# When the second piece of q and the first weight slice are sent for, in a fused attention and SwiGLU kernel

## The chip, the cores and the metric

The kernel runs on one core of a Trainium2 chip. The metric is the device time of one execution in microseconds (us), and the median of several executions is what kernels are compared by. The profile shows one execution in detail.

## The reference

Attention without a softmax over pairs: q is normalised along its 64 features, k along the sequence, and the two products are taken with the small matrix in the middle. The result, as 4608 tokens of 512 features, goes through a SwiGLU block.

```python
# q, k, v: (8 batches, 8 heads, 576 positions, 64 features), float32
q_s = softmax(q, axis=features);  k_s = softmax(k, axis=positions)
kv  = einsum('bhsd,bhse->bhde', k_s, v)
x   = einsum('bhsd,bhde->bhse', q_s, kv)        # -> (4608, 512)
g   = x @ w_gate                                # (512, 1536)
out = (g * sigmoid(g) * (x @ w_val)) @ w_out    # (1536, 512), float32 out
```

## The kernel before

**Tiling.** The eight heads of a batch are two groups (G = 0 and 1) of four. One load brings q, k or v of one batch and group into a tile of 128 partitions with 2 x 576 float32 each (576 KB). Positions are cut into nine steps of 64; `A` is steps 0 to 4 and `Z` is steps 5 to 8. For batch 0 alone, q is loaded in these two pieces: first A (320 KB a group), later Z (256 KB a group). The weights `wg`, `wv` and `wo` are cast to float16 as they are loaded. `wg` and `wv` come in four slices of columns each: 256, 256, 512 and 512 wide. I call the eight slices w0 to w7 in the order of issue: w0 is the first of `wg`, w1 the first of `wv`, w2 the second of `wg`, and so on. The list `w_dma` of the code holds them.

**Queues.** The order on every engine is written by hand (`tc.manual_schedule()`), and each engine takes its instructions in that order. All loads of q, k and v are issued by SyncE, one after the other, on one hardware queue (q1 in the profile). The weight slices are issued by GpSimd on a software queue (q0), since they are cast on the way. Both queues are served by the same 16 DMA engines. `load(b, G, what, src, after, t0, t1)` issues one load; if `after` is given, SyncE waits until that other transfer has landed before it issues this one. `tc.add_manual_dep(a, b, ...)` does the same for any pair of instructions.

**The start.** SyncE issues, with nothing to wait for: q piece A for both groups, k and v of group 0, k and v of group 1, q piece Z for both groups. GpSimd waits for k of group 0 to land and then issues w0 to w7 one behind the other. SyncE's next load, q of batch 1, waits for w5.

While this comes in, TensorE is kept running by products of zeros (`warm_up`). ScalarE takes the exponential of q's piece A (line 129, tile `eq`) and of k (line 129, tile `ek`); VectorE and GpSimd normalise q (`rs`, `rr` at lines 148 and 153, `qs` at line 160); TensorE transposes q (line 176, `tp` copied to `qt`), forms `kv` (line 200) and then `x` (line 245, `xp`), which is copied to `xt` as the input of the SwiGLU block.

**The first chunk.** `PLAN_0` is a string of steps that says what every engine does next. It begins:

```
zq0 zs0 zq1 zs1 zn1* M00 zn0 N00 M10 N10 M20 zt0* M30 zt1 zx0 zx1 N20 N30 M01 M11
```

`zq0` and `zq1` are the exponentials of q's piece Z for group 0 and 1, on ScalarE. `zs` are its sums (VectorE), `zn` the multiplications (`zn1*` on VectorE, `zn0` on GpSimd), `zt` the transposes (`zt0*` is copied by ScalarE, `zt1` by VectorE), and `zx` the products with `kv`. `Mm0` is the gate product (`g_ps`, line 318) of the weight columns 128 m to 128 m + 127 with the tokens of piece A, followed by a Silu on ScalarE (`sg`, line 331); `Nm0` is the value product (`u_ps`, line 318) followed by a multiplication on VectorE (`hr`, line 336). `Mm1` and `Nm1` are the same for the tokens of piece Z. So M00 needs w0, N00 needs w1, M20 needs w2, N20 needs w3, and M01 needs what `zx` made. The name `psp` is the pool of eight banks of PSUM that all products share.

**Afterwards** come seven chunks of 512 tokens. TensorE runs their products (lines 398, 451, 489 and 543) nearly without a pause. `w_out` comes in four slices: two of them wait for w6, two (step `wo` of the plan) for v of batch 1.

Of the kernel before, what the change touches and what calls it, by code (L numbers as in the profile page):

```python
# [12 lines left out]
SYNC = mybir.DependencyInfo(mybir.DependencyClass.Sync, mybir.DependencyReason.DATA)  # L13
# [3 lines left out]
def kernel(  # L17
# [59 lines left out]
    dmas = {}  # L77
    raw = {}

    def load(b, G, what, src, after=None, t0=0, t1=T):  # L80
        if t0 == 0:
            raw[what, b, G] = ld.tile(
                [128, 2, T * 64], FP32, tag=what, name=what, bufs=3 if what == "q" else None
            )
        ap = bass.AP(
            tensor=src.tensor,
            offset=src[b, 4 * G].offset + 64 * t0,
            ap=[[T * 64, 128], [2 * HSTR, 2], [1, 64 * (t1 - t0)]],
        )
        d = nc.sync.dma_start(out=raw[what, b, G][:, :, 64 * t0:64 * t1], in_=ap)  # L90
        if after is not None:
            tc.add_manual_dep(d.ins, after.ins.name, SYNC, reason="order of loads")
        dmas[what, b, G] = d
# [5 lines left out]
    def w_slice(dst, src, c0, n):  # L99
        ap = bass.AP(  # L100
            tensor=src.tensor,
            offset=src[0, c0].offset,
            ap=[[d_ff, 128], [128 * d_ff, KT], [1, n]],
        )
        return nc.gpsimd.dma_start(out=dst[:, :, c0:c0 + n], in_=ap)
# [17 lines left out]
    A, Z = BANKS = ((0, 5), (5, 9))  # L123
# [488 lines left out]
    with tc.manual_schedule():  # L612
# [3 lines left out]
            load(0, G, "k", k)  # L616
            load(0, G, "v", v)
        for G in range(NG):
            load(0, G, "q", q, None, *Z)
        warm = const.tile([128, 1], FP32, name="warm", tag="warm")  # L620
        nc.vector.memset(warm, 0.0)
        nc.scalar.activation(out=warm, in_=warm, func=AF.Exp)
# [14 lines left out]
        w_dma = []  # L637
        for c0, n in ((0, 256), (256, 256), (512, 512), (1024, 512)):
            w_dma.append(w_slice(wg, moe_w_gate, c0, n))
            w_dma.append(w_slice(wv, moe_w_val, c0, n))  # L640
        tc.add_manual_dep(w_dma[0].ins, dmas["k", 0, 0].ins.name, SYNC, reason="order of loads")
        load(1, 0, "q", q, after=w_dma[5])
        load(1, 1, "q", q)

# [205 lines left out]
```

## Time and profile before

| what | us |
|---|---|
| median of 6 runs | 297.14 |
| lowest and highest of these | 296.86 and 299.57 |
| the profiled execution, its time | 297.63 |
| the profiled execution, its span | 295.6 |
| TensorE busy in the span | 284.9 (96%) |
| VectorE busy | 236.7 (80%) |
| ScalarE busy | 216.2 (73%) |
| GpSimd busy | 149.2 (50%) |

The span runs from the first to the last instruction of the core; the time holds some 2 us more that lie around it. Times in a view are counted from the start of the span. In the profile PE is TensorE, PEld its weight loads, ACT is ScalarE, DVE is VectorE, POOL is GpSimd, and SPq is SyncE's issuing of DMAs. An arrow `<-` in a group's name stands between what is written and what is read; an arrow in front of an engine names what ended its waiting.

### The profile page before, as it was taken

How to read it: one execution, taken by the hardware profiler on the slowest of the kernel's cores; microseconds unless marked ns; L12 is line 12 of the kernel's file. 1: busy time of each engine (PE TensorE's matmuls, PEld its weight loads, DVE VectorE, ACT ScalarE, POOL GpSimd, SP SyncE). 2: the span in 40 equal slices, each digit the busy share in tenths (PEclk: the TensorE clock that was granted, in tenths of full speed). 3: DMA queues.
4: the chain of work that ended last, by engine and by line, in shares of the span. 5: the costliest groups of instructions: out<-in, count | busy, mean ns of one | idle time of the engine just before them, and what ended most of it. 6: DMA issues, size and time to landing. Idle time of an engine off the chain costs nothing.

```text
span 295.6 us, 7115 instructions
## 1 busy us (share of the span) xinstructions
PE 284.9 (96%) x2708; PEld 233.3 (79%) x2708; DVE 236.7 (80%) x523; ACT 216.2 (73%) x401; POOL 149.2 (50%) x128
## 2 busy tenths in 40 slices
PE   8889999799999999999999999999999999999993
PEld 6658775577888878887888788878887888888882
DVE  3475797598998889888988898889888798677791
ACT  4674896798896799669966997599758766677421
POOL 2813688466329722972197219730973255344300
PEclk9999999999999999999999999999999999999999
DMA  7999999757906970698059805990570000510065
GB/s 220 323 201 246 283 329 268 250 109 193 358 12 147 265 295 0 133 252 321 1 121 249 335 4 122 225 357 2 111 113 2 2 2 0 109 35 2 0 145 142
DMA packets 39425, 46.46 MB, mean 157 GB/s; under 512 B 16352, under 2 KB 23008, under 8 KB 39392
## 3 DMA queue, kind: packets, MB, share of 16 engines
q1 hardware_dynamic: 33408, 41.03, 49.1%
q0 software_dynamic: 5824, 4.72, 10.3%
q8 instruction: 21, 0.34, 0.5%
q10 hardware_dynamic: 160, 0.26, 0.2%
q14 instruction: 12, 0.10, 0.1%
HBM read 37.75 MB, written 9.44 MB: 160 GB/s over the span
## 4 chain that ended last, share of the span: by engine, by line
PE 83%; DMA 10%; DVE 2%; POOL 2%; ACT 1%; issue 1%; SPq 0%; ACTq 0%; DVEq 0%
PE sx L398 24%; PE ox L543 13%; PE sw L398 12%; PE ow L543 6%; PE sy L398 6%; DMA wo<-in_moe_w_out_dram 5%; PE oy L543 4%; PE g_ps L318 3%; PE u_ps L451 3%; PE g_ps L451 3%; PE u_ps L318 3%; DMA wv<-in_moe_w_val_dram 3%; PE kv L200 2%; DMA k<-in_k_dram 2%; PE o_ps L489 1%; POOL qs L160 1%
## 5 line engine op out<-in xcount | busy, mean ns | idle before, releaser
L398 PEld LDWEIGHTS <-gt 128*128 128x128 f16 x672 | 65.3, 98 | 10.8 <-issue 0.6
L433 POOL TENSOR_TENSOR hr<-sg,u 128x512 bf16<-128x512 f16 (+1 forms) x32 | 36.6, 1144 | 73.1 <-ACT sg L424 47.7
L117 ACT COPY s<-sx 128x512 f32<-128x512 f32 (+1 forms) x70 | 40.7, 581 | 17.0 <-PE sx L398 16.9
L398 PE MATMUL sx<-xs,gt 128*128 128x256 f16 (+1 forms) x336 | 49.9, 271 | 0.1
L442 POOL TENSOR_TENSOR hr<-sg,u 128x512 bf16<-128x512 f16 (+1 forms) x32 | 36.5, 1141 | 23.5 <-ACT sg L441 23.5
L543 PEld LDWEIGHTS <-hs 128*128 128x128 bf16 x384 | 37.4, 98 | 5.5
L437 DVE TENSOR_TENSOR u<-sx,s 128x512 f16<-128x512 f32 (+1 forms) x42 | 28.5, 679 | 12.9 <-PE sx L398 5.6
L398 PEld LDWEIGHTS <-wg 128*128 128x128 f16 x336 | 32.4, 98 | 5.2 <-issue 0.2
L160 POOL TENSOR_TENSOR qs<-eq,rr 128x1152 bf16<-128x1152 bf16 (+2 forms) x15 | 30.7, 2052 | 11.3 <-DVE rr L153 7.7
L432 DVE TENSOR_TENSOR u<-sw,s 128x512 f16<-128x512 f32 (+1 forms) x42 | 28.5, 679 | 7.5 <-PE sw L398 7.3
L441 ACT ACTIVATE sg<-sx 128x512 f16<-128x512 f32 (+1 forms) x42 | 25.0, 596 | 10.8 <-PE sx L398 10.0
L424 ACT ACTIVATE sg<-s 128x512 f16<-128x512 f32 (+1 forms) x42 | 26.6, 632 | 6.8 <-DVE s L422 6.7
L543 PEld LDWEIGHTS <-hr 128*128 128x128 bf16 x288 | 28.2, 98 | 3.3
L422 DVE TENSOR_TENSOR s<-sy,s 128x512 f32<-128x512 f32 (+1 forms) x42 | 27.8, 661 | 2.5 <-PE sy L398 1.3
L117 ACT COPY s<-sw 128x512 f32<-128x512 f32 (+1 forms) x36 | 21.0, 582 | 6.1 <-PE sw L398 5.8
L398 PE MATMUL sy<-xt,wg 128*128 128x256 f16 (+1 forms) x168 | 24.9, 271 | 0.1
L148 DVE TENSOR_REDUCE rs<-eq 128x18 f32<-128x1152 bf16 (+2 forms) x18 | 21.7, 1203 | 4.2 <-ACT eq L129 4.2
L398 PE MATMUL sx<-xt,wg 128*128 128x256 f16 (+1 forms) x168 | 25.0, 271 | 0.0
L398 PE MATMUL sw<-xs,gt 128*128 128x256 f16 (+1 forms) x168 | 24.9, 271 | 0.0
L398 PE MATMUL sx<-xt,gt 128*128 128x256 f16 (+1 forms) x168 | 24.9, 271 | 0.0
L398 PE MATMUL sw<-xs,wv 128*128 128x256 f16 (+1 forms) x168 | 24.7, 271 | 0.0
L543 PE MATMUL ox<-wt,hs 128*128 128x256 f16 x192 | 23.6, 273 | 0.0
(107 smaller groups left out, 548.9 us busy)
## 6 DMA issues: line engine op xcount, KB each, us to landing
k<-in_k_dram SPq DMA_DIRECT2D x16, 576.0 KB, 7.4
v<-in_v_dram SPq DMA_DIRECT2D x16, 576.0 KB, 8.0
out_dram<-o_sb SPq DMA_DIRECT2D x70, 128.0 KB, 2.4
q<-in_q_dram SPq DMA_DIRECT2D x14, 576.0 KB, 7.0
wo<-in_moe_w_out_dram POOLq DMA_DIRECT2D x4, 384.0 KB, 9.0
wg<-in_moe_w_gate_dram POOLq DMA_DIRECT2D x2, 512.0 KB, 12.3
wv<-in_moe_w_val_dram POOLq DMA_DIRECT2D x2, 512.0 KB, 14.8
q<-in_q_dram SPq DMA_DIRECT2D x2, 320.0 KB, 3.5
```

The source lines that it names most:

```text
L117: nc.scalar.copy(out=out, in_=in_)
L148: nc.vector.reduce_sum(out=s["rs"][:, r], in_=s["eq"].rearrange("p t h d -> p (t h) d")[:, r], axis=mybir.AxisListType.X,)
L160: eng.tensor_mul(s["qs"].rearrange("p t (h d) -> p (t h) d", d=64)[:, r], s["eq"].rearrange("p t h d -> p (t h) d")[:, r], s["rr"][:, r].t ...
L398: nc.tensor.matmul(out=bank[:, h * j:h * j + h], lhsT=wgt(kk, j), rhs=rhs[:, kk, 0:h], start=first and j == 0 and kk == 0, stop=kk == 1, s ...
L422: nc.vector.tensor_add(self.s1, self.y[:, 0:w], self.s1)
L424: nc.scalar.activation(out=self.sa[:, 0:w], in_=self.s1, func=AF.Silu)
L432: nc.vector.tensor_add(u, self.w[:, 0:w], self.s2)
L433: meng.tensor_mul(self.out(0), self.halves(self.sa), self.halves(u))
L437: nc.vector.tensor_add(self.u, self.x[:, 0:w], self.s5)
L441: nc.scalar.activation(out=sb[:, 0:w], in_=self.x[:, 0:w], func=AF.Silu)
L442: meng.tensor_mul(self.out(1), self.halves(sb), self.halves(self.u))
L543: nc.tensor.matmul(out=dst[p][:, 0:HN], lhsT=lhs(kk, p), rhs=rhs(kk), start=start and i == 0, stop=i == HM - 1, skip_group_check=True,)
```

## The change

Two triggers are changed. SyncE now issues q's piece Z of group 0 only when k of group 1 has landed; the piece Z of group 1 follows in SyncE's order. GpSimd issues w0, and with it the seven slices behind it, when v of group 0 has landed, where it was k of group 0. The order of the instructions on each engine is unchanged, and so is every transfer.

```diff
@@ load order of batch 0 @@
             load(0, G, "k", k)
             load(0, G, "v", v)
         for G in range(NG):
-            load(0, G, "q", q, None, *Z)
+            load(0, G, "q", q, dmas["k", 0, 1], *Z)
...
-        tc.add_manual_dep(w_dma[0].ins, dmas["k", 0, 0].ins.name, SYNC, reason="order of loads")
+        tc.add_manual_dep(w_dma[0].ins, dmas["v", 0, 0].ins.name, SYNC, reason="order of loads")
```

## The prediction

> **What bounds the kernel now.** I read the page first. TensorE is busy for 96% of the span, and in the chain that ended last it holds 83%, DMA 10%. So a change of two load triggers can matter only where TensorE still waits for loads, near the start. I therefore took the chain of waits over the first 24 us, in order of time (start, duration, what):
>
> ```profile
> 1.75 5.98 DMA k<-in_k_dram
> ...
> 8.04 0.93 POOL wg L105
> 8.97 7.66 DMA wv<-in_moe_w_val_dram
> 16.62 0.05 issue
> 16.67 0.72 PE u_ps L318 x4
> 17.39 0.54 PE g_ps L318 x4
> ```
>
> The reader is to see that the end is set through k of group 0, then w0's issue, then w1's landing at 16.62, then N00 on TensorE. From there the chain stays on TensorE with no piece of DMA until 41.39, where a slice of `w_out` comes in. What is late at 16.67 is thus late at the end, unless something behind it has room.
>
> Next the timeline of ScalarE around that point (start, duration, group, idle before and its releaser), since the exponentials of q's piece Z stand ahead of the first Silu:
>
> ```profile
> 15.10 0.42 ACT L117 CAST xt<-xp 128x320 f16<-128x320 f32 x1 [0.67 <-PE xp L245]
> 15.42 1.15 ACT L129 ACTIVATE eq<-q 128x512 bf16<-128x512 f32 x2
> 16.59 1.28 ACT L331 ACT_TABLE_LOAD   x1
> 17.88 0.77 ACT L331 ACTIVATE sg<-g_ps 128x320 f16<-128x320 f32 x2
> 19.05 0.44 ACT L331 ACTIVATE sg<-g_ps 128x320 f16<-128x320 f32 x1 [0.41 <-PE g_ps L318]
> 19.39 0.58 ACT L117 COPY qt<-tp 128x512 bf16<-128x512 bf16 x1
> ```
>
> Neither exponential waits for its data now: the pieces land 9.4 and 10.1 us after their issues at 3.80 and 4.31, at 13.2 and 14.4, and are wanted at 15.42 and about 16.0. ScalarE's only slack behind them is the 0.41 ahead of 19.05.
>
> Last, GpSimd, and the DMAs by stretches of one us (the last two columns are the DMA share and GB/s):
>
> ```profile
> 8.04 0.94 POOL L105 DMA_DIRECT2D wg<-in_moe_w_gate_dram  x1 [0.73 <-DMA k<-in_k_dram]
> ...
> 13.36 0.80 POOL L105 DMA_DIRECT2D wv<-in_moe_w_val_dram  x1
> 17.16 1.04 POOL L160 TENSOR_TENSOR qs<-eq,rr 128x512 bf16<-128x512 bf16 x1 [3.00 <-DVE rr L153]
> ```
>
> ```profile
> 11.00:12.00 1.00, 1.00 (x19) 0.82 (x14) 0.58 (x3) 1.00 (x1) 1.00 (x3) 1.00 1.09 368
> 12.00:13.00 1.00, 0.73 (x8) 0.26 (x5) 0.56 (x3) 0.90 (x4) 1.00 (x2) 1.00 1.33 257
> 13.00:14.00 1.00, 0.88 (x21) 0.76 (x22) 0.59 (x4) 0.39 (x2) 1.00 (x2) 1.00 1.41 207
> 26.00:27.00 1.00, 1.00 (x11) 0.80 (x9) 0.94 (x3) 0.73 (x3) 0.00 (x0) 1.00 1.24 206
> 27.00:28.00 1.00, 1.00 (x11) 0.83 (x9) 0.42 (x2) 0.68 (x2) 0.71 (x1) 1.00 1.19 281
> ```
>
> The GB/s are bytes written. Near 390 means float32 loads of k, v and q; near 206 means weights, whose float16 writes are half of what is read. The change of rate shows who is served: weights begin only near 11.7 although w0 was issued at 8.04, that is, when the loads queued ahead of them are nearly through. The engines are busy throughout, so the change can only reorder this work or open a hole in it.
>
> **The triggers.** k of group 1 is issued at 2.77 and takes 8.1: the first Z load moves from 3.80 to about 10.95 and the second to about 11.45, by the 0.51 between two of SyncE's issues. SyncE's next load, q of batch 1, waits for w5 until 24.2 anyway, so nothing else is held up in its queue. v of group 0 is issued at 2.26 and takes 7.2, so it is there at 9.45 (ScalarE's cast starts then), where k was there at 7.73. All eight weight issues move by 1.7 us, and the last ends near 15.9 instead of 14.16. What stands behind them on GpSimd is zn0 at 17.16, after 3.00 idle: that covers it with 1.3 to spare. Without the cover it would cost TensorE's transposes the excess.
>
> **What does not get better.** k and v of both groups are ahead of the Z loads in one queue, and weights flow only near 11.7, when k of group 1 (10.9) has landed and v of group 1 (3.29 + 9.1 = 12.4) nearly has. So taking the Z loads and the weights out of their way buys nothing that I can find in these rows.
>
> **Step 1, w1 and N00.** Upper end: the 7.66 us from issue to landing stays, w1 lands at 18.3, and N00 is 1.7 late. Lower end: weights start as soon as v of group 1 is drained, hence near 11.7 as before, and the 512 KB of q (1.3 us at 390) are no longer all ahead of them; w1 could be 1.3 earlier, but TensorE waits only 0.67 there, so -0.67. I take the middle, +0.5: the queue that kept the weights from starting is gone earlier, but there is a hole, since k and v run out near 11.7 to 12.4 while q's first bytes can't come before about 12.3 (the first load is issued at 0.74 and bytes flow in the stretch from 2 to 3). M00, which needs w0, isn't the tighter one: its last operand from `xt` comes at 15.62.
>
> **Step 2, the Z loads.** They now arrive at engines that hold queued weights. The nearest row is the pair of q loads of batch 1, issued at 24.22 and 24.70 into queued w6 and w7. The rate stays at 206 until 27, so first bytes come some 3.0 us after the issue; the second load takes 8.1 and lands at 32.8. That is 1152 KB in the remaining 5.6 us, or 206 KB/us, half the unloaded rate. For 512 KB: 10.95 + 3.0 + 2.5 = 16.45. I add one small slice's time, 0.75 us of issue, since slices are queued here once per 0.75 us but land only every 1.35 (w2 at 9.71 + 8.1, w3 at 10.44 + 8.7), so that the queue is still growing. So the second piece lands near 17.2 where zq1 would have started at 16.0: 1.2 late. ScalarE takes its work in order; the table load, the first Silus and the copy of `qt` behind zq1 are all 1.2 late, less the 0.41 of slack, and zx0 on TensorE, which stands right behind that copy, is 0.8 late. Bounds: 14.7 to land (the 320 KB load at 0.74 took 3.3 us unloaded), which costs nothing; or the 8.1 us of the row unscaled, 19.55, which makes 3.55 late and costs 3.1.
>
> The Trainium skill, page "DMA: Bandwidth & Descriptors", section on queues, rings and completion order, says that an engine alternates between queues a packet at a time, about 9 to 17 descriptors. By that rule the q pieces would share evenly from 12.3 on and take an estimated 2.6 us, to 14.9, and step 2 would cost nothing. The row at 24.22, with its 3 us without a byte of q, speaks against so short a wait, though 206 KB/us afterwards fits an even share.
>
> **The sum.** Both steps delay the same engine and don't add up: the larger counts. Step 1 gives +0.5, step 2 gives +0.8, so +0.8. All later loads follow from landings or from TensorE's own progress and move along. The profiled execution would go from 297.63 to 298.4 (span 295.6 to 296.4); it lies 0.5 above the median of 297.14, so the median becomes 297.9.
>
> **Rivals.**
> - *The Z pieces are held behind the weights* (slower). The queue of slices keeps q out for longer than the row at 24.22 shows. For: the weights are issued first, and ScalarE can't pass zq1. Against: in that row q got its half once it started. If q lands with w3, 19.1 + 0.5, zq1 is 3.6 late and TensorE 3.2: 300.3. It decides from a landing of the second piece at about 17.9, where the loss passes 1.5. Chance 0.25.
> - *The weights keep their latency* (slower). Step 1's upper end, +1.7: 298.8. For: nothing in this trace shows a weight slice starting sooner after its issue. Against: the work queued ahead explains that start. Chance 0.13.
> - *Everything hidden*: the pieces share evenly, w1 lands where it did: 297.1 to 297.5. Chance 0.12.
> - *The weights gain* (faster): N00 loses its wait of 0.67, 296.5. Beyond that only the 1.83 us that TensorE waits at 54.83 for `w_out` could go too, if the later loads fall better: 294.6. Against: the second needs an order of transfers that the change doesn't touch. Chance 0.11, of which 0.06 passes the bound below.
>
> The forecast itself has 0.39, with its own range of 297.3 to 298.7.
>
> **How the numbers follow.** A difference of 0.5%, 1.5 us, is about what a measurement of this kernel can tell from no change. Faster by more: 0.06. Slower by more: all of the first rival, most of the second (0.11), and the forecast's upper edge (0.08), together 0.44. Within: 0.50. For the range I leave out the gain beyond 296.6 (about 0.08) and the part of the first rival beyond 300.2 (about 0.12).
>
> **What would show it.** In the profile of the changed kernel: the w0 issue at about 9.75; q's Z issues near 10.95 and 11.45; ScalarE waiting before `eq` for a DMA of q, which it does not now; N00 at 16.7 to 18.3; and the same distance from N00 to the end. I am wrong if `eq` has no wait and N00 comes no later than 16.67, if the Z pieces land after 18, or if the distance from N00 to the end changes by over 0.5 us.

## The result, and the profile after

The changed kernel takes 298.77 us (median of 28 runs, 296.85 to 301.89), the kernel before 297.12 (65 runs). The ratio is 1.0049, with a 95% interval of 1.0034 to 1.0064: slower by 1.5 us, which lies so near to the 0.5% that was called the bound of no change that the interval can't say on which side. The ratio leaves out the few executions that took over 1.5% more than the fastest of the same kernel; the two medians, which are 1.65 us apart, do not. The profiled execution took 299.21 with a span of 297.2; before it was 297.63 and 295.6.

The chain of waits of the changed kernel (start, duration, what) no longer runs over w1 and N00. It runs over k of group 1, SyncE, and q's second piece:

```profile
2.77 8.66 DMA k<-in_k_dram
...
11.46 0.37 SPq L90
11.82 0.04 issue
11.87 7.32 DMA q<-in_q_dram
19.18 0.02 issue
19.21 0.63 ACT eq L129
19.84 0.02 issue
19.85 1.28 ACT L331
21.14 0.01 issue
21.15 1.09 ACT sg L331 x3
22.24 0.49 ACT qt L117
22.73 0.04 issue
22.77 0.42 PE xp L245 x8
23.19 1.19 PE u_ps L318 x8
```

The last line is N20, which began at 20.83 before: 2.36 late. The chain of the kernel before had this from there on:

```profile
20.83 1.19 PE u_ps L318 x8
...
36.58 1.06 ACT sg L331 x3
37.64 3.00 POOL qs L160
40.64 0.74 POOL wo L113
41.39 13.40 DMA wo<-in_moe_w_out_dram
54.83 0.81 PE o_ps L489 x3
```

ScalarE's timeline shows the waits that were not there before, 0.59 and 1.70 ahead of the two exponentials of piece Z:

```profile
15.86 0.42 ACT L117 CAST xt<-xp 128x320 f16<-128x320 f32 x1 [0.67 <-PE xp L245]
16.88 0.63 ACT L129 ACTIVATE eq<-q 128x512 bf16<-128x512 f32 x1 [0.59 <-DMA q<-in_q_dram]
19.21 0.63 ACT L129 ACTIVATE eq<-q 128x512 bf16<-128x512 f32 x1 [1.70 <-DMA q<-in_q_dram]
```

zq1 starts at 19.21 instead of 16.0. On TensorE N00 is late too, but the chain does not run over it:

```profile
18.04 0.72 PE L318 MATMUL u_ps<-xt,wv 128*128 128x320 f16 x4 [1.26 <-DMA wv<-in_moe_w_val_dram]
...
22.77 0.42 PE L245 MATMUL xp<-qt,kn 64*64 64x256 bf16 x8 [0.80 <-ACT qt L117]
```

GpSimd issues w0 at 10.28, 2.2 later than before. Of this 1.7 is the trigger. The rest is not the change's: the first loads, issued at the same times in both, landed later here. ScalarE's start on k of group 0 is at 8.48 instead of 7.75 (between 7.5 and 8.7 in the profiles of this study), on v of group 0 at 10.00 instead of 9.45, and on k of group 1 at 11.46 instead of 10.93. So about 0.5 us of all the times above belong to this one execution.

Later in the chain a part is given back at the wait for `w_out`:

```profile
43.02 0.75 POOL wo L113
43.77 12.64 DMA wo<-in_moe_w_out_dram
56.41 0.04 issue
56.45 0.81 PE o_ps L489 x3
```

GpSimd's issue is 2.38 later than before (40.64), but the slice takes 12.64 instead of 13.40 to land, and TensorE goes on at 56.45 instead of 54.83, 1.62 later. That is what is left at the end of the span, 1.6.

### The profile page after: what moved, and what is told of

Its sections match the earlier page's. It is cut to its first block, busy times and chain, and to the rows that moved or that the text cites. A ratio compares the mean times of both kernels' runs of the same rounds, so it can differ in the third digit from the quotient of the medians.

```text
span 297.2 us, 7114 instructions
## 1 busy us (share of the span) xinstructions
PE 286.1 (96%) x2708; PEld 233.6 (79%) x2708; DVE 236.9 (80%) x523; ACT 216.2 (73%) x401; POOL 149.2 (50%) x128
## 4 chain that ended last, share of the span: by engine, by line
PE 81%; DMA 10%; DVE 2%; ACT 2%; POOL 1%; SPq 1%; issue 0%; ACTq 0%; DVEq 0%
PE sx L398 24%; PE ox L543 13%; PE sw L398 12%; PE ow L543 6%; PE sy L398 6%; DMA wo<-in_moe_w_out_dram 4%; PE oy L543 4%; PE u_ps L451 3%; PE g_ps L451 3%; DMA k<-in_k_dram 3%; PE g_ps L318 3%; DMA q<-in_q_dram 2%; PE u_ps L318 2%; PE kv L200 2%; PE o_ps L489 1%; POOL qs L160 1%
## 5 line engine op out<-in xcount | busy, mean ns | idle before, releaser
L148 DVE TENSOR_REDUCE rs<-eq 128x18 f32<-128x1152 bf16 (+2 forms) x18 | 21.8, 1210 | 6.0 <-ACT eq L129 6.0
```

Source lines behind the costliest of these rows:

```text
L148: nc.vector.reduce_sum(out=s["rs"][:, r], in_=s["eq"].rearrange("p t h d -> p (t h) d")[:, r], axis=mybir.AxisListType.X,)
```

## The experiments

Two theories stood at the start. Theory Z: the loss is ScalarE's wait for q's second piece, which the weights hold back. Theory W: the loss is that the weights come later. All kernels below are compared with the kernel before, run on the same chip.

**The q trigger alone.** The weights are issued on k of group 0, as before.

```diff
-            load(0, G, "q", q, None, *Z)
+            load(0, G, "q", q, dmas["k", 0, 1], *Z)
```

> The q trigger alone; the weights are issued on k of group 0 as before. Theory Z (the loss is ScalarE's wait for q's second piece, held back by weights queued in the DMA engines): the weights are queued even earlier than in the changed kernel, so the piece lands at 18 or later, ScalarE waits 2 us or more before its exponential of group 1, and the loss is all there: 298.3 to 299.3, 0.4 to 0.7% over before. Theory W (the loss is the later issue of the weights): N00 on TensorE starts at 16.7 or earlier and the time is that of before, 297.1, or up to 0.6 less.

Measured: 300.19 us (6 runs), ratio 1.0089 (1.0057 to 1.0120). The second piece lands 7.9 us after its issue, at 18.9, and ScalarE waits for both pieces. N00 starts at 15.73, 0.94 earlier than before, so the weights gain and the kernel loses: theory W falls. But the loss is larger than the changed kernel's although zx0 is no later (22.50). The stretches of one us of this run show why; the third column from the right is the clock granted to TensorE:

```profile
20.00:21.00 1.00, 0.70 (x8) 0.53 (x8) 0.93 (x3) 0.99 (x2) 0.25 (x1) 1.00 1.23 204
21.00:22.00 1.00, 0.64 (x6) 0.33 (x5) 0.90 (x3) 1.00 (x4) 0.00 (x0) 0.88 1.25 208
22.00:23.00 1.00, 0.50 (x8) 0.25 (x7) 0.56 (x3) 0.82 (x3) 0.00 (x0) 0.50 1.24 207
23.00:24.00 1.00, 1.00 (x8) 0.59 (x5) 0.75 (x2) 0.61 (x2) 0.00 (x0) 0.50 1.23 203
...
27.00:28.00 1.00, 1.00 (x7) 0.69 (x6) 0.00 (x0) 0.40 (x2) 0.35 (x1) 0.50 1.25 209
28.00:29.00 1.00, 1.00 (x8) 0.78 (x7) 0.13 (x1) 0.37 (x1) 1.00 (x2) 0.70 1.13 316
```

TensorE paused 1.93 us ahead of zt0 and 0.80 ahead of zx0, and from about 21.8 to 28.6 it has half its clock. Five of the six executions had a mean clock of 0.988 to 0.992 and took 299.4 to 300.9; the sixth kept 0.999 and took 297.5. I had not thought of this.

**The weight trigger alone.**

```diff
-        tc.add_manual_dep(w_dma[0].ins, dmas["k", 0, 0].ins.name, SYNC, reason="order of loads")
+        tc.add_manual_dep(w_dma[0].ins, dmas["v", 0, 0].ins.name, SYNC, reason="order of loads")
```

> The weight trigger alone; q's second piece is issued at 3.8 as before. Theory Z: the piece lands by 14.5, ScalarE has no wait for it, and the time is within 0.25% of before, 296.7 to 297.7, with N00 at 16.7 to 17.3. Theory W: N00 comes 1.4 us later than before, at 18.0, and the time is 298.5, all of the change's loss.

Measured: 297.08 us (12 runs), ratio 0.9989 (0.9966 to 1.0013): no loss, as theory Z has it. The profile, of the slowest of the twelve (299.46), has N00 at 18.20, 1.53 later than before, but its first loads were 0.9 late; that leaves some 0.6 for the trigger, which does not show in the median. This interval lies wholly below the changed kernel's (1.0034 to 1.0064). The two kernels differ in q's trigger alone, so the loss needs that trigger.

**Both triggers on v of group 0.** q's second piece is issued some 1.5 us earlier than in the changed kernel; the weights stay as changed.

```diff
-            load(0, G, "q", q, dmas["k", 0, 1], *Z)
+            load(0, G, "q", q, dmas["v", 0, 0], *Z)
```

> Both triggers on v of group 0: q's second piece now waits for the same landing as the weights, 1.5 us earlier than in the changed kernel. Theory Z: its bytes start about 1.3 us after SyncE's issue, near 10.8, ahead of the first weight bytes near 11.7, so the pieces land by 14 to 15, ScalarE has no wait, and the time is 297.0 to 297.6. Theory W: the weights are as late as in the changed kernel and the time is 298.5.

Measured: 297.86 us (12 runs), ratio 1.0021 (1.0001 to 1.0041), a little above what was expected of theory Z and well below the 298.5 of W. Its interval and the changed kernel's overlap slightly. The pieces are issued at 9.29 and 9.7 and land 4.0 and 4.5 us later, ahead of the weights; ScalarE runs both exponentials without a wait:

```profile
15.48 1.15 ACT L129 ACTIVATE eq<-q 128x512 bf16<-128x512 f32 x2
```

So a second piece that was issued at 9.7, beside w0 (9.58), took 4.5 us, and one that was issued at 11.87, 1.6 behind w0 (10.28), took 7.3.

**The changed kernel without the wait.** The exponential reads the steps of piece A instead.

```diff
-            in_=raw[what, b, G].rearrange("p h (t d) -> p t h d", d=64)[:, t0:t1],
+            in_=raw[what, b, G].rearrange("p h (t d) -> p t h d", d=64)[:, t0 % 5:t0 % 5 + t1 - t0],
```

> The changed kernel, but the exponential of q's second piece reads the first piece's steps instead, so it waits for no late load; all transfers stay, and only the numbers of positions 320 to 575 of batch 0 differ. Theory Z: the wait at 19.2 is gone, zx0 on TensorE goes back to within 0.3 us of N00's own lateness, and at most the lateness of N00 is left: 297.3 to 298.0. Theory W: nothing changes, 298.5.

Measured: 299.09 us (6 runs), ratio 1.0068 (1.0044 to 1.0093). Both theories missed: with the wait gone the kernel is no faster. TensorE's timeline shows what took its place:

```profile
15.21 1.02 PE L318 MATMUL g_ps<-xt,wg 128*128 128x320 f16 x4
18.36 1.25 PE L318 MATMUL u_ps<-xt,wv 128*128 128x320 f16 x4 [2.12 <-DMA wv<-in_moe_w_val_dram]
19.40 1.27 PE L318 MATMUL g_ps<-xt,wg 128*128 128x320 f16 x4
20.46 1.27 PE L318 MATMUL u_ps<-xt,wv 128*128 128x320 f16 x4
21.53 0.76 PE L318 MATMUL g_ps<-xt,wg 128*128 128x320 f16 x4
```

After a pause of 2.12 us the same four products take 1.25 us instead of 0.72, until 21.7. The granted clock, again the third column from the right, is half meanwhile:

```profile
18.00:19.00 1.00, 0.65 (x3) 0.41 (x4) 0.94 (x2) 0.53 (x2) 0.43 (x1) 0.60 1.42 196
19.00:20.00 1.00, 1.00 (x6) 0.52 (x5) 0.29 (x1) 0.00 (x0) 0.00 (x0) 0.50 1.28 206
20.00:21.00 1.00, 1.00 (x6) 0.52 (x5) 0.20 (x1) 0.29 (x1) 0.00 (x0) 0.50 1.26 205
21.00:22.00 1.00, 1.00 (x7) 0.64 (x6) 0.16 (x1) 0.14 (x1) 0.00 (x0) 0.69 1.24 201
```

This called for a third theory, C: a pause of some 2 us costs TensorE its clock, and a part of the loss is that.

**Theory C, three kernels.** A step `wu` issues products of zeros, as the kernel's own `warm_up` does, where TensorE would pause.

In the changed kernel (the kernel that ran has nine products ahead of N00, where the expectation says eight):

```diff
-... M00 zn0 N00 M10 N10 M20 zt0* M30 zt1 zx0 ...
+... M00 wu9 zn0 N00 M10 N10 M20 zt0* M30 zt1 wu6 zx0 ...
```

> The changed kernel with products of zeros in TensorE's pauses: 8 (0.86 us at full clock) between M00 and N00 and 6 ahead of zx0. Theory C (a part of the change's loss is TensorE's clock, which falls to half for some microseconds in those executions where the pauses last long enough): no execution has a mean clock under 0.995 any more, and the time falls by 0.3 to 1.0 us against the changed kernel, to 297.7 to 298.4. Rival (the loss is the waits alone): 298.6 as the changed kernel.

Measured: 298.83 us (9 runs), ratio 1.0072 (1.0042 to 1.0101). The mean clock was 0.994 to 0.999, so it was kept, but the time did not fall: for the changed kernel theory C fails, and its loss is not mainly the clock. Its own runs say the same: of the 27 executions in the ratio, nineteen had a mean clock of 0.994 or more and a median of 298.45, and eight had 0.990 to 0.993 and a median of 298.98. In this profile the second piece lands at 19.4 and zx0 starts at 23.02, behind the same chain as in the changed kernel.

In the kernel without the wait for q:

```diff
-... M00 zn0 N00 ...
+... M00 wu14 zn0 N00 ...
```

> The changed kernel without the wait for q's second piece (the exponential reads the first piece's steps), and with 14 products of zeros (1.5 us) between M00 and N00. Theory C: the half-clock stretch from 18.4 to 21.7 us of the run without them is gone, the mean clock is 0.995 or more, and the time falls by 1 to 1.5 us to 297.3 to 298.1, between the kernel before and the changed one. Rival: the late weights cost what they cost, 299.1 as without the products.

Measured: 298.15 us (12 runs), ratio 1.0036 (1.0015 to 1.0058), 0.9 us less than without the products, where theory C had 1 to 1.5. The two intervals overlap, the clocks do not: all twelve executions had a mean of 0.995 or more, where five of six had 0.989 to 0.992 without the products. N00 starts at 18.05 and its four products take 0.72 again.

In the kernel with the q trigger alone:

```diff
-... M20 zt0* M30 zt1 zx0 ...
+... M20 wu14 zt0* M30 zt1 wu6 zx0 ...
```

> The q trigger alone, with 14 products of zeros ahead of zt0 and 6 ahead of zx0, where TensorE paused 1.93 and 0.80 us. Theory C: the half-clock stretch from 21.8 us on is gone and the time falls from 300.2 to about 298.0, near the one execution of that kernel that kept its clock (297.5). Rival: 299.5 to 300.2.

Measured: 298.42 us (7 runs), ratio 1.0050 (1.0029 to 1.0070), down from 1.0089, with mean clocks of 0.995 to 0.999. The intervals overlap (1.0057 to 1.0070), but the median fell by 1.8 us and the half-clock stretch is gone. Read from the two ratios, and as an estimate, the 0.9% of the q trigger alone is some 0.5% of waits and some 0.4% of clock. The changed kernel pauses in shorter pieces (1.26, 0.30 and 0.80 us in its profile), and that profile shows full clock throughout.

**Fewer weights ahead of q.** The q trigger alone, with the third and later weight slices issued only when the second piece has landed.

```diff
+        tc.add_manual_dep(w_dma[2].ins, dmas["q", 0, 1].ins.name, SYNC, reason="order of loads")
```

> The q trigger alone, but the third and later weight slices are issued only when q's second piece has landed. Read for landings, not for time. Theory Q (the piece is held by the weights queued ahead of it): with only two slices queued the second piece lands by 16, 2.5 us or more earlier than the 18.9 of the q trigger alone, and ScalarE waits less than 0.5 us for it. Rival (it is late because of the trigger and the transfer themselves): it lands near 18.9 again.

Measured, in one execution (302.74 us, mean clock 0.986): the pieces are issued at 11.70 and 12.1, a us later than in the q trigger alone because the first loads were late, and the second lands 5.5 us after its issue instead of 7.9. ScalarE waits 0.76 and then runs both exponentials in one go. The landing at 17.6 misses the expected 16, by 1.06 of the 1.6 through the late issue, and the wait misses the 0.5; the shortening by 2.4 us is near the 2.5 of theory Q. The DMA view by halves of a microsecond shows where the time goes. The two pieces are 544 packets on queue q1, with no other load on it by then:

| kernel | the pieces are issued at | first packets | most packets | landing |
|---|---|---|---|---|
| changed | 11.46, 11.87 | 13.5 to 14.0 | 491 by 17.0 | 19.18 |
| q trigger alone | 10.64, 11.0 | 14.0 to 14.5 | 520 by 18.0 | 18.9 |
| this one | 11.70, 12.1 | 13.5 to 14.0 | 487 by 16.0 | 17.6 |

So the pieces start later and come more slowly the more weights are queued ahead. But the last tenth is slow as well: some 2 us in the changed kernel, and some 1.5 here, where no weight was on the engines from 15.5 to 19. What holds these last packets the runs don't show.

**Without the wait, weights first.** The q trigger alone, and the exponential reading piece A as above: nothing needs the late piece, and TensorE has its weights early.

```diff
-            load(0, G, "q", q, None, *Z)
+            load(0, G, "q", q, dmas["k", 0, 1], *Z)
...
-            in_=raw[what, b, G].rearrange("p h (t d) -> p t h d", d=64)[:, t0:t1],
+            in_=raw[what, b, G].rearrange("p h (t d) -> p t h d", d=64)[:, t0 % 5:t0 % 5 + t1 - t0],
```

> The q trigger alone with the exponential of q's second piece reading the first piece's steps, so that nothing waits for the late piece: the weights have the engines to themselves and N00 starts near 15.7, 0.9 us earlier than before, without pauses that lower the clock. Theory Q (the whole loss of the q trigger is the wait for the second piece): the 0.9% over before is gone, 296.2 to 297.2. Rival (the trigger also costs elsewhere, as in the later loads): 298 or more.

Measured: 297.31 us (12 runs), ratio 1.0008 (0.9979 to 1.0038), 0.1 us outside the expected band and not to be told from before. The 0.9% of the q trigger alone is the wait for the piece with what follows from it, as far as an interval of 0.3% to either side can tell. N00's early start brings nothing either: the third slice now shares the engines with q, and M20 waits for it.

```profile
17.53 0.71 PE L318 MATMUL u_ps<-xt,wv 128*128 128x320 f16 x4
19.86 0.72 PE L318 MATMUL g_ps<-xt,wg 128*128 128x320 f16 x4 [1.62 <-DMA wg<-in_moe_w_gate_dram]
```

**How much of a delay at N00 reaches the end.** The kernel before, with every load as it was, but 18 products of zeros ahead of N00.

```diff
-... M00 zn0 N00 ...
+... M00 wu18 zn0 N00 ...
```

> The kernel before with 18 products of zeros (1.93 us at full clock) between M00 and N00, so that N00 starts near 18.0 instead of 16.67, as late as in the changed kernel, with every load as before and no pause that could lower the clock. Theory R (lateness at N00 reaches the end one to one): 298.4. Theory S (a part is given back where TensorE waits 1.83 us for w_out at 54.83): 297.1 to 297.8.

Measured: 297.45 us (12 runs), ratio 1.0010 (0.9984 to 1.0037). N00's group starts at 18.32 and N20 at 22.46, 1.6 later than before. In the median 0.36 us of it are left, and at the end of this profile's span 0.5. The chain of this run shows where the rest went:

```profile
42.29 0.75 POOL wo L113
43.04 12.31 DMA wo<-in_moe_w_out_dram
55.35 0.04 issue
55.39 0.81 PE o_ps L489 x3
```

GpSimd's issue is 1.65 later than before, the landing only 0.56. I read this as the slice sharing the engines with other loads, which are further along when it starts later; no run tests it. TensorE's wait there is 1.0 instead of 1.83. So one to one (theory R) falls: a delay of 1.6 us on TensorE alone, with every load at its time, is mostly absorbed at the wait for `w_out`.

**Two tries for a faster kernel.** The kernel before, with the first slices cut in two:

```diff
-        for c0, n in ((0, 256), (256, 256), (512, 512), (1024, 512)):
+        for c0, n in ((0, 128), (128, 128), (256, 256), (512, 512), (1024, 512)):
```

(The four places that count slices are moved by two.)

> The kernel before with the first slice of each weight cut into two of 128 columns, so that N00 needs half the bytes. w1 lands before 16.0 and N00 loses its wait of 0.67 us. Theory R: 296.5. Theory S: 297.1, no gain, or a loss if the narrower descriptors (256 bytes written each) are slow.

Measured: 297.42 us (12 runs), ratio 1.0002 (0.9974 to 1.0029). N00 starts at 15.91, 0.76 earlier, but M20 then waits 0.34 for its slice and zx0 is only 0.26 earlier. The next slice has taken the place of the first.

And with one multiplication moved from GpSimd to VectorE:

```diff
-... Q01 Q11* nd1:1* ek0:1 ...
+... Q01 Q11* nd1:1 ek0:1 ...
```

> The kernel before with one multiplication of batch 1's q moved from GpSimd (3.0 us) to VectorE (1.3 us), so that GpSimd issues the last two slices of w_out up to 0.7 us earlier. It is a try for a faster kernel: 296.4 if TensorE's wait at 54.83 shrinks by that much, 297.1 to 298 if VectorE's 1.3 us delay TensorE instead.

Measured: 300.67 us (6 runs), ratio 1.0116 (1.0076 to 1.0157), clearly slower, by more than expected. The multiplication stands late in VectorE's order and takes 2.71 us there, and TensorE waits 3.2 us for it; behind the pause the granted clock is half again:

```profile
42.00:44.00 2.00, 0.22 (x2) 0.00 (x0) 2.00 (x3) 0.56 (x1) 1.69 (x1) 1.00 1.17 244
44.00:46.00 2.00, 0.56 (x9) 0.56 (x9) 1.45 (x2) 0.00 (x0) 2.00 (x2) 0.95 1.08 240
46.00:48.00 2.00, 2.00 (x23) 1.19 (x22) 1.02 (x5) 1.64 (x2) 2.00 (x2) 0.50 1.11 278
```

No kernel of this study is measurably faster than the one before.

## Why the prediction was right or wrong, point by point

- **The verdict.** 297.9 was forecast, with 0.50 for no change beyond 0.5% and 0.44 for slower; 298.77 was measured, a ratio of 1.0049. The direction was right, and the chain of the changed kernel runs over step 2. The size was 0.8 and is 1.5. That the number is no further off is in part luck: two errors, below, have opposite signs. Of the signs of being wrong that were named, one came: the second piece landed after 18. The other two did not: `eq` waits, and from N00 to the end it is 279.2 us instead of 278.9.
- **The triggers** came as worked out: w0 at 10.28 and q at 11.46 and 11.87 instead of 9.75, 10.95 and 11.45, all 0.5 later through the first loads. GpSimd's cover held: its zn0, at 18.62, waits 2.21 for VectorE and not for the issues.
- **Step 1, the weights.** The +0.5 at N00 was measured as +1.37, of which 0.5 is the late first loads; w1 lands 7.7 us after w0's issue, 8.6 before. The term is 0.9, inside its bounds. The lower end, in which the weights gain when q is not ahead of them, was seen in the q trigger alone: 0.94 earlier, which is the wait of 0.67 and some 0.3 of earlier first loads.
- **Step 2, the late piece.** This is the term that was mis-sized. I took the 16.45 that the batch 1 loads gave and added one slice's issue, for a landing of 17.2, 6.25 us after SyncE's first issue. It landed at 19.18, 7.7 us after. The start was about right (first packets between 13.5 and 14.0, where 10.95 + 3.0 had 13.95), and 491 of the 544 packets were there by 17.0. The landing waits for the last 53, for which the sum had nothing but one slice's issue time of 0.75. The row had two slices queued, here eight were being queued; the kernel that held back six of them shortened the transfer by 2.4. The path behind it was right: the table load, the Silus, the copy of `qt`, then zx0. zx0 is 2.75 late for 3.2 at zq1, against 0.41 of slack forecast.
- **The first rival** (held behind the weights, deciding from a landing at 17.9) is what happened by the landing, but not by its price. It asked 3.2 us for a landing at 19.6; 2.36 us were late at N20 for 19.18, and 1.6 at the end.
- **"What is late at 16.67 is thus late at the end"** was wrong as a rule, and so was the reading under it that the chain stays on TensorE until 41.39. It leaves TensorE at 36.58 for ScalarE and GpSimd, whose issue at 40.64 sets when the slice of `w_out` is sent for; a delay has to pass through that transfer. 0.74 of the 2.36 was given back at the wait for `w_out`, and 18 products of zeros, which made N20 1.6 late, cost 0.10% with an interval that holds zero. I had seen that wait of 1.83 us and used it only in the rival that gains. The two errors, a piece 2 us later and a delay that is partly absorbed, have opposite signs.
- **The second rival** (weights keep their latency, +1.7) and theory W fall with the weight trigger alone, 0.9989.
- **What was missing** is the clock. No case of the prediction had a price for TensorE losing its clock around a pause, and in the q trigger alone it is, by the estimate above, nearly half of the loss. In the changed kernel, products of zeros kept the clock and brought no time back.

What stays open: how much of the changed kernel's 1.5 us is ScalarE's wait. In the q trigger alone the loss went with the wait (1.0008). In the changed kernel it did not: without the wait, and with the clock kept, it is still at 1.0036 (1.0015 to 1.0058), which overlaps with 1.0049 (1.0034 to 1.0064). This is just above the weight trigger alone (0.9966 to 1.0013), from which it differs in q's late bytes, which nothing waits for, and in the products of zeros. As far as intervals that barely miss each other can tell, late weights together with late bytes of q cost something where neither does alone (1.0008 for the late bytes), and the runs don't say on which way it reaches the end. The artificial delay (0.9984 to 1.0037), with N20 as late, overlaps with both.

## What to carry to other kernels

A load that is triggered late does not only start late: in these runs it also took longer behind what had been queued meanwhile on the same engines (7.3 us instead of 4.5). So ask what will be queued at the moment of the trigger, and count to the landing of the last packet. Then follow a delay past the next wait that has room before calling it a loss. Last, look at how long TensorE will pause: around 2 us without products cost it half its clock in two of these kernels.

## What the runs showed of the hardware that I had not expected

- A pause of 2.12 us on TensorE ended in half the granted clock from about 18.2 to 21.6, and the same four products took 1.25 us instead of 0.72. In the q trigger alone the clock fell only at about 21.8, 1.5 us after the pause of 1.93 had ended, and stayed at half until 28.6: 6.8 us, twice the 3.4 of the other. Somewhat shorter pauses kept the clock, such as the 1.83 ahead of 54.83 in the kernel before. The Trainium skill, page "TensorE: Matmul & The Clock Gate", Part 1, says that the clock halves after at least one idle window of about 3.4 us, in a window that runs free of the kernel; here a little over 2 us without a product was enough in the profiled execution, and five of that kernel's six had a low mean clock, so the measurement sets the shorter bound.
- The 512 KB of q's second piece took from 11.46 to 19.18 behind queued weights and 9.29 to 14.2 ahead of them. In the changed kernel the windows of one microsecond (length, busy time of PE, PEld, DVE, ACT and POOL, granted clock, DMA share, GB/s) begin with a hole, when k and v had nearly run out and the weights and q had hardly begun to arrive:

```profile
11.00:12.00 1.00, 0.79 (x20) 0.68 (x20) 0.06 (x1) 0.69 (x2) 1.00 (x3) 1.00 0.31 111
12.00:13.00 1.00, 1.00 (x12) 0.72 (x10) 0.58 (x4) 0.94 (x3) 1.00 (x2) 1.00 0.92 115
13.00:14.00 1.00, 0.38 (x8) 0.16 (x8) 1.00 (x2) 0.88 (x2) 1.00 (x2) 1.00 1.44 224
```

The DMA share is 0.31 from 11 to 12, and the rate doubles from 13 on. The hole that the prediction's first step named is there. It does not explain the piece's longer transfer by itself: from 12.5 to 13.5 the DMA view has packets of weights alone, and the piece's first packets come after that.
- The landing of the first loads varies: k of group 0, issued at 1.75 in every kernel here, started its users between 7.5 and 8.7. A single profile is no measure of half a microsecond at the start.
